# One PSUM bank of row segments for all output terms, and ten projection rows loaded behind the last V block

## The chip, the cores and the metric

The kernel runs on one core of one Trainium2 chip. The metric is the device time of a whole execution in microseconds (us). A "span" is the time from the first to the last instruction of one profiled execution; it is about 1.7 us shorter than the time of the same run. Positions such as "393.2" are microseconds from the start of the span. "Granted clock" is the share of full speed that the profile shows for TensorE's clock: 0.50 is called half clock below. PSUM is the memory in which matmul results accumulate.

## The reference, cut to what matters

One token of a decode step: grouped-query attention over a cache of 65,536 positions, plus an MLP, plus the residual.

```python
def _A_ref(x, k_cache, v_cache, wq, wo):          # x: 1x1x1024, caches: 1x4x65536x128, 32 query heads
    q = (x @ wq) ...
    p = softmax(q @ k * Dh**-0.5)                  # 8 query heads share one K/V head
    o = p @ v
    return o.reshape(B, Sq, 4096) @ wo             # wo: 4096x1024, 32 "rows" of 128x1024, one per query head
def _B_ref(x, w1, w2, w3, w4):
    ... x1 = x + hs                                # w1, w2: 1024x1024
    return x1 + _gelu(_layernorm(x1) @ w3) @ w4    # w4: 3584x1024
x = A_x; xn = _layernorm(x)
return x + _A_ref(xn, ...) + _B_ref(xn, ...)       # 1x1x1024, bf16
```

Nearly all of the work is to read 170 MB once: K and V are 134 MB of it.

## The kernel before

The caches come in 32 blocks (four K/V heads with eight blocks each) of 2 MB of K and 2 MB of V. All loads are issued by SyncE into one queue. Each engine keeps a list of operations, and a small bookkeeping class derives the waits: an operation waits for whoever last wrote what it reads, and for whoever last wrote or read what it writes. It does not ask whether that was the engine itself; the argument below comes back to this.

```python
def _deps(q, reads, writes):
    for b in reads:
        for s, v in b.w.items():
            q.wait((s, v))
    for b in writes:
        for s, v in b.w.items():
            q.wait((s, v))          # also when s is the engine's own semaphore
        for s, v in b.r.items():
            q.wait((s, v))
```

After the last block of a K/V head, `combine_1` and `combine_2` sum and normalise its eight heads into `OTh_bf`. Then each head's vector (128x1) meets its projection row (128x1024), eight matmuls with 128x128 weights and one moving column each:

```python
def wo_pe(h, g, src=None):
    ...
    for ncx in range(KT_D):                        # KT_D = 8
        fns.append(lambda e, ...: e.matmul(OA_ps[:, ncx:ncx + 1], view[:, ncx * P:(ncx + 1) * P], OTh_bf[:, h, g:g + 1],
                                           start=(g == 0 and ncx == 0), stop=(g == G - 1), skip_group_check=True))
    _grp(q_pe, fns, reads=bufs + [b_OTh[h]], writes=[b_OA], partial=(g > 0))
    if g == G - 1:  acc += OA_ps                   # on VectorE
```

The last ten projection rows (two of the third K/V head, all eight of the fourth) load into slots that the MLP's w3 has left free, two for each of blocks 25 to 29. The K and V loads run three blocks ahead, so six of these rows go into the queue ahead of the last K block (issued in block 28). The w4 weights (seven chunks of 1 MB, four 128-row slices each) load last, into freed slots. The end of the program:

```python
for i in range(len(wo_tail)):
    at(min(t_ws_free + i // 2, t0), "dma", lambda i=i: issue_wo_tail_row(i))
... # the 32 blocks, the last combine
for (h_, g_) in wo_tail:
    wo_pe(h_, g_, src=wo_tail_src[(h_, g_)])
mm_interleaved(H2_ps, 0, KT_D, chunks_of("w4"), ...)          # 7 groups of 32 one-column matmuls
fin = acc + H2_ps; transpose fin on TensorE; cast to orow     # 8 partitions x 128
ev_out = _dma(q_sp, ch_out, lambda e: e.dma_start(out=out[0, 0, :].rearrange("(kt p) -> kt p", p=P), in_=orow[:, :]), ...)
```

Of the kernel before, what the change touches and what calls it, by code (L numbers as in the profile page):

```python
# [6 lines left out]
BF = mybir.dt.bfloat16  # L7
F32 = mybir.dt.float32
ACTF = mybir.ActivationFunctionType
ALU = mybir.AluOpType  # L10
# [83 lines left out]
def _op(q, fn, reads=(), writes=(), partial=False):  # L94
    _deps(q, reads, writes)
    ev = q.op(fn, True)
    _done(ev, reads, writes, partial)
    return ev


def _grp(q, fns, reads=(), writes=(), partial=False):
    _deps(q, reads, writes)
    ev = None
    for i, fn in enumerate(fns):
        ev = q.op(fn, i == len(fns) - 1)
    _done(ev, reads, writes, partial)
    return ev
# [8 lines left out]
def _dma(q, chan, fn, reads=(), writes=(), partial=False):  # L116
    _deps(q, reads, writes)
    chan.n += 1
    ev = q.dma(fn, chan.sem, 16 * chan.n)
    _done(ev, reads, writes, partial)  # L120
    return ev
# [10 lines left out]
def bass_parallel_sum__gqa_block_cached__mixer_s_mlp__decode_kernel(  # L132
# [13 lines left out]
    P = 128  # L146
    D = A_x.shape[2]
    HKV, SK, DH = A_k_cache.shape[1], A_k_cache.shape[2], A_k_cache.shape[3]
    HQD = A_wq.shape[1]
    HQ = HQD // DH  # L150
    G = HQ // HKV
    F = B_w3.shape[1]
    KT_D = D // P
# [10 lines left out]
    with ExitStack() as es:  # L164
# [3 lines left out]
        def sb(name, shape, dt):  # L168
            return E(nc.sbuf_tensor(name, shape, dt))

        def ps(name, shape, dt):
            return E(nc.psum_tensor(name, shape, dt))
# [59 lines left out]
        ge_b = sb("ge_b", [P, KT_F], F32)  # L232
        h1g_bf = sb("h1g_bf", [P, KT_D], BF)
        gh_bf = sb("gh_bf", [P, KT_F], BF)
        fin = sb("fin", [P, KT_D], F32)
        orow = sb("orow", [KT_D, P], BF)

        H3_ps = ps("H3_ps", [P, 512], F32)
        H2_ps = H3_ps[:, 32:64]
        OA_ps = ps("OA_ps", [P, 512], F32)  # L240
        S_ps = ps("S_ps", [P, 512], F32)
        PT_ps = ps("PT_ps", [P, 512], F32)
        MBB_ps = ps("MBB_ps", [P, 512], F32)
# [19 lines left out]
        b_Kn = [[_B(), _B()] for _ in range(NK)]  # L263
        b_Vn = [[_B(), _B()] for _ in range(NV)]
        b_X = [[_B() for _ in range(4)] for _ in range(2)]
        b_H3 = _B(); b_H2 = _B(); b_tmpO = [_B(), _B()]
        b_S = _B(); b_PT = _B(); b_MB = _B(); b_OT = _B()
        b_M0 = _B(); b_M1 = _B()
        b_mrow = [_B(), _B()]; b_R = [_B(), _B()]
# [3 lines left out]
        b_Oacc = _B(); b_brun = [_B(), _B()]; b_dd = [_B(), _B()]; b_ff = [_B(), _B()]  # L273
        b_WS = [[_B() for _ in range(4)] for _ in range(NWS)]
        b_wo = [_B() for _ in range(NWO)]
        b_OA = _B()
        b_cb = _B()
        b_OTh = [_B() for _ in range(HKV)]
        b_acc = _B()
# [62 lines left out]
        for kt in range(KT_D):  # L342
# [3 lines left out]
        _op(q_pe, lambda e: e.matmul(M0_ps[:, 160:160 + KT_D], x8[:, :], ident_bf[0:KT_D, 0:KT_D], start=True, stop=True),  # L346
            reads=[b_x8, b_const], writes=[b_M0])
        _op(q_dve, lambda e: e.tensor_copy(xT[:], M0_ps[:, 160:160 + KT_D]), reads=[b_M0], writes=[b_xT])

        ln_uid = [0]  # L350

# [29 lines left out]
        def mm_interleaved(ps_tile, col0, ncols, chunks, rhs_fn, b_rhs, b_ps, kt0=0, nkt_total=None):  # L381
            nkt = nkt_total if nkt_total is not None else sum(c[2] for c in chunks)
            first = (kt0 == 0)
            kt = kt0
            for sl, lhs_fn, kts in chunks:
                fns = []
                for kk in range(kts):
                    for ncx in range(ncols):
                        fns.append(lambda e, kk=kk, ncx=ncx, kt=kt, st=(first and kk == 0 and ncx == 0), lhs_fn=lhs_fn:
                                   e.matmul(ps_tile[:, col0 + ncx:col0 + ncx + 1], lhs_fn(kk, ncx), rhs_fn(kt + kk),  # L390
                                            start=st, stop=(kt + kk == nkt - 1), skip_group_check=True))
                _grp(q_pe, fns, reads=sl.bufs + [b_rhs], writes=[b_ps], partial=not first)
                first = False
                kt += kts
# [152 lines left out]
        def wo_pe(h, g, src=None):  # L547
            if src is None:
                ws_ = (h * G + g) % NWO
                view, bufs = wo_sb[:, ws_, :], [b_wo[ws_]]  # L550
            else:
                view, bufs = src
            fns = []
            for ncx in range(KT_D):
                fns.append(lambda e, ncx=ncx, g=g, h=h, view=view: e.matmul(OA_ps[:, ncx:ncx + 1], view[:, ncx * P:(ncx + 1) * P], OTh_bf[:, h, g:g + 1],  # L555
                                                                          start=(g == 0 and ncx == 0), stop=(g == G - 1), skip_group_check=True))
            _grp(q_pe, fns, reads=bufs + [b_OTh[h]], writes=[b_OA], partial=(g > 0))
            if g == G - 1:
                _op(q_dve, lambda e: e.tensor_tensor(out=acc[:], in0=acc[:], in1=OA_ps[:, 0:KT_D], op=ALU.add), reads=[b_OA, b_acc], writes=[b_acc])

        def mk_loads(name, w, nkt, per):
            ncol = w.shape[1]
# [32 lines left out]
        def chunks_of(name):  # L595
            res = []
            for ld in loads_early + loads_mid + loads_late:
                if ld["name"] != name:
                    continue
                sl, ncol = ld["slot"], ld["ncol"]  # L600
                if name == "w3":
                    res.append((sl, (lambda kk, ncx, sl=sl: sl.view[:, 512 * (ncx // 4) + (ncx % 4): 512 * (ncx // 4) + (ncx % 4) + 4 * P: 4]), 1))
                else:
                    res.append((sl, (lambda kk, ncx, sl=sl, ncol=ncol: sl.view[:, kk * ncol + ncx * P: kk * ncol + (ncx + 1) * P]), ld["kts"]))
            return res

        b_h1 = _B(); b_x1 = _B(); b_xn3 = _B(); b_gh = _B(); b_fin = _B(); b_orow = _B()

        def mlp_early_1():
            mm_interleaved(M1_ps, 64, KT_D, chunks_of("w1"), lambda kt: xn2I_bf[:, kt:kt + 1], b_xn2I, b_M1)  # L610
# [2 lines left out]
        def mlp_early_2():  # L613
            mm_interleaved(M1_ps, 72, KT_D, chunks_of("w2"), lambda kt: g_bf[:, kt:kt + 1], b_const, b_M1)
            _op(q_dve, lambda e: e.tensor_tensor(out=x1[:], in0=xn[:], in1=M1_ps[:, 72:72 + KT_D], op=ALU.add), reads=[b_xn, b_M1], writes=[b_x1])
            _op(q_dve, lambda e: e.tensor_tensor(out=acc[:], in0=acc[:], in1=M1_ps[:, 72:72 + KT_D], op=ALU.add), reads=[b_acc, b_M1], writes=[b_acc])
            layer_norm(x1, b_x1, xn3, xn3_bf, b_xn3)
# [14 lines left out]
        def at(period, slot, fn):  # L632
            pending.setdefault(period, []).append((slot, fn))
# [17 lines left out]
        for i, ld in enumerate(loads_early):  # L651
            at(2 + i // 2, "dma", lambda ld=ld, i=i: issue_load(ld, slots["ws"][i % NWS]))
        at(7, "c", lambda: mlp_early_1())
        at(8, "c", lambda: mlp_early_2())
        for j, ld in enumerate(loads_mid):
            wave, jj = divmod(j, NWS)
            at(10 + 6 * wave + jj, "dma", lambda ld=ld, jj=jj: issue_load(ld, slots["ws"][jj]))
# [8 lines left out]
        def issue_wo_tail_row(i):  # L666
            h_, g_ = wo_tail[i]
            sl = slots["ws"][i // 4]
            j = i % 4
            _dma(q_sp, ch_wot[i], lambda e, sl=sl, j=j, h_=h_, g_=g_: e.dma_start(out=sl.view[:, j * D:(j + 1) * D],  # L670
                                                                                 in_=A_wo[(h_ * G + g_) * DH:(h_ * G + g_ + 1) * DH, :]),
                 writes=[sl.bufs[j]])
            wo_tail_src[(h_, g_)] = (sl.view[:, j * D:(j + 1) * D], [sl.bufs[j]])
            wo_tail_next[0] = max(wo_tail_next[0], i + 1)

        t0 = max(NBLK - KA, NBLK - VA, t_ws_free, 0)
        for i in range(len(wo_tail)):
            at(min(t_ws_free + i // 2, t0), "dma", lambda i=i: issue_wo_tail_row(i))
        at(t0, "dma", lambda: issue_late(slots["ws"][3:4]))
        for n in range(max(0, NBLK - NK), NBLK):  # L680
            at(max(n, t0), "dma", lambda n=n: issue_late(slots["k"][n % NK]))
# [4 lines left out]
        for n in range(NBLK):  # L686
            h, nb = divmod(n, NB)
            issue_k(n + KA)
            issue_v(n + VA)
            run_pending(n, "dma")  # L690
            QK(n)
            Ttr(n + 1, [0])
            stats1(n)
            run_pending(n, "a")
            MB(n)
            stats2(n)
            EXP(n)
            Ttr(n + 1, [1])
            run_pending(n, "b")
            PTr(n)  # L700
            PTevac(n)
            Ttr(n + 1, [2, 3])
            PV(n)
            FLASH(n)
            run_pending(n, "c")
            if nb == NB - 1:
                at(n + 1, "a", lambda h=h: combine_1(h))
                at(n + 1, "b", lambda h=h: combine_2(h))

# [6 lines left out]
                issue_wo_tail_row(i)  # L716
        while late_next[0] < len(loads_late):
            issue_late(slots["ws"])
        for (h_, g_) in wo_tail:
            wo_pe(h_, g_, src=wo_tail_src[(h_, g_)])  # L720
        mm_interleaved(H2_ps, 0, KT_D, chunks_of("w4"), lambda kt: gh_bf[:, kt:kt + 1], b_gh, b_H2)
        _op(q_dve, lambda e: e.tensor_tensor(out=fin[:], in0=acc[:], in1=H2_ps[:, 0:KT_D], op=ALU.add), reads=[b_acc, b_H2], writes=[b_fin])
        _op(q_pe, lambda e: e.transpose(out=M0_ps[0:KT_D, 300:300 + P], in_=fin[:, :], identity=ident_f[:, :]), reads=[b_fin, b_const], writes=[b_M0])
        _op(q_dve, lambda e: e.tensor_copy(orow[:, :], M0_ps[0:KT_D, 300:300 + P]), reads=[b_M0], writes=[b_orow])
        ev_out = _dma(q_sp, ch_out, lambda e: e.dma_start(out=out[0, 0, :].rearrange("(kt p) -> kt p", p=P), in_=orow[:, :]), reads=[b_orow])
        q_sp.wait(ev_out)

        block.sync(lambda e: q_sp.emit(e))
# [32 lines left out]
```

## Time and profile before

| | before |
|---|---|
| time, median of 3 runs | 413.93 us (413.74 to 414.36) |
| span of the profiled run | 412.0 us |
| bytes moved, mean rate | 170 MB, 413 GB/s |
| last K block landed | 376.8 |
| last head's vectors ready | 397.0 |
| last w4 matmul ended | 409.4 |

The page shows the span in 40 equal slices. The first line is the busy share of the DMA engines in tenths, the second the rate in GB/s.

```profile
DMA  7999999999999999999999999999999999999990
GB/s 280 426 435 430 433 429 431 424 437 425 431 433 428 428 429 429 427 421 436 430 426 429 431 425 427 426 433 428 425 431 428 431 429 426 425 422 421 423 387 13
```

The stream of transfers is full all the time, and its end sets a floor. Finer stretches of the end of the stream (stretch, its length, then each engine's busy time, the granted clock of TensorE, the DMA share, GB/s):

```profile
399.50:400.00 0.50, 0.35 (x14) 0.29 (x11) 0.00 (x0) 0.00 (x0) 0.00 (x0) 0.50 0.74 311
401.50:402.00 0.50, 0.50 (x25) 0.50 (x23) 0.16 (x1) 0.00 (x0) 0.00 (x0) 0.50 0.42 180
402.50:403.00 0.50, 0.35 (x15) 0.38 (x15) 0.00 (x0) 0.00 (x0) 0.00 (x0) 0.50 0.00 0
```

The rate falls from 399 on, with the busy share of the 16 DMA engines (0.74, then 0.42), and reaches zero after 402.5. The chain of work that ended last (start, duration, what) tells what comes after:

```profile
352.46 24.32 DMA Kn<-in_A_k_cache_dram
...
394.87 1.88 PE M_ps L543 x8
...
400.66 0.14 issue
400.80 0.36 PE OA_ps L555 x8
...
407.08 0.14 issue
407.21 1.00 PE H_ps L390 x32
...
409.67 0.39 PE M_ps L723
```

The softmax of the last block hangs on the last K block (landed at 352.46 + 24.32 = 376.8). The combine's matmuls (`M_ps`) end at 396.75; ten projection rows (`OA_ps`) follow at 0.36 us and a gap of 0.14 us each, and seven w4 chunks (`H_ps`) at 1.00 and 0.14 us. From 402.5 to the end at 412.0 nothing is transferred but the output. The issuing engine's timeline (start, duration, engine, line, operation) shows where the six rows stand in the queue:

```profile
345.38 6.97 SPq L670 DMA_DIRECT2D WS<-in_A_wo_dram  x2
352.46 3.08 SPq L424 DMA_DIRECT2D Kn<-in_A_k_cache_dram  x1
...
410.39 0.31 SPq L725 DMA_DIRECT2D out_dram<-orow  x1
```

Two rows (the fifth and sixth) were issued directly ahead of the last K block. Their issue took 7 us, against 0.3 to 0.5 us elsewhere; I read this as a full queue.

### The profile page before, as it was taken

Reading aid. Unit: us, or ns where it says so; the run is one execution under the profiler, and the core shown is the slowest. Engines: PE = TensorE matmul, PEld = TensorE weight load, DVE = VectorE, ACT = ScalarE, POOL = GpSimd, SP = SyncE. Lnnn points to the kernel's source line nnn. Section 1 sums busy time; section 2 is a strip of 40 time slices with the busy share of each in tenths; the row PEclk is TensorE's granted clock in tenths of the full one; section 3 lists DMA queues with packets and bytes.
Section 4 is the critical chain, followed back from the end, with each engine's and each line's share of the span. In section 5 each row is a group of like instructions: output and inputs, shape, how many; then the busy total and the mean of one; then the engine's idle time right before and its main releaser. Section 6 shows DMA issues by size and latency. Waiting matters only on the chain.

```text
span 412.0 us, 5690 instructions
## 1 busy us (share of the span) xinstructions
PE 194.8 (47%) x2237; PEld 84.4 (20%) x2237; DVE 226.0 (55%) x401; ACT 48.4 (12%) x127; POOL 61.4 (15%) x88
## 2 busy tenths in 40 slices
PE   1532444434157656424465453445457544333666
PEld 1521111101014312101123121112224111011156
DVE  1037766736476588644456664445666766655400
ACT  0000211201011021110111110011111111011100
POOL 4000011111011121111110011111110111111210
PEclk9999999995555556566555555655555566656555
DMA  7999999999999999999999999999999999999990
GB/s 280 426 435 430 433 429 431 424 437 425 431 433 428 428 429 429 427 421 436 430 426 429 431 425 427 426 433 428 425 431 428 431 429 426 425 422 421 423 387 13
DMA packets 18043, 170.25 MB, mean 413 GB/s; under 512 B 2272, under 2 KB 2272, under 8 KB 7392
## 3 DMA queue, kind: packets, MB, share of 16 engines
q1 hardware_dynamic: 18016, 169.88, 97.5%
q8 instruction: 18, 0.29, 0.3%
q14 instruction: 9, 0.07, 0.0%
HBM read 169.87 MB, written 0.00 MB: 412 GB/s over the span
## 4 chain that ended last, share of the span: by engine, by line
DMA 56%; DVE 18%; PE 11%; SPq 7%; issue 4%; ACT 3%; POOL 1%; POOLq 0%; ACTq 0%; DVEq 0%
DMA Kn<-in_A_k_cache_dram 51%; DVE X L449 10%; DMA X<-in_A_wq_dram 5%; SPq L670 4%; ACT p_sb L491 2%; DVE pT_f L508 2%; DVE mrow L468 2%; PE PT_ps L503 2%; PE S_ps L461 2%; PE H_ps L390 2%; PE M_ps L543 1%; PE OT_ps L516 1%; SPq L436 1%; PE OA_ps L555 1%; SPq L344 1%
## 5 line engine op out<-in xcount | busy, mean ns | idle before, releaser
L449 DVE STREAM_TRANSPOSE X<-Kn 128x1024 f32<-128x1024 f32 x128 | 153.6, 1221 | 104.2 <-DMA Kn<-in_A_k_cache_dram 104.1
L516 PE MATMUL OT_ps<-Vn,pT_f 128*32 128x512 bf16 x512 | 60.7, 627 | 25.9 <-DVE pT_f L508 25.9
L461 PE MATMUL S_ps<-X,Yall 128*32 128x512 bf16 x512 | 59.0, 607 | 11.4 <-DVE X L449 10.1
L474 PE MATMUL MBB_ps<-Rm,Lmat 128*128 128x16 bf16 x32 | 6.2, 195 | 109.8 <-DVE Rm L469 109.8
L530 POOL TENSOR_TENSOR O_acc<-O_acc,tmpO 128x513 f32<-128x513 f32 x28 | 32.9, 1175 | 89.9 <-ACT tmpO L524 89.9
L491 ACT ACTIVATE p_sb<-S_ps,brun 128x512 bf16<-128x512 f32 x32 | 22.0, 687 | 188.9 <-DVE brun L489 168.9
L528 POOL TENSOR_SCALAR O_acc<-O_acc,ff 128x513 f32<-128x513 f32 x28 | 19.5, 698 | 164.0 <-ACT ff L497 164.0
L503 PE MATMUL PT_ps<-p_sb,permR 128*128 128x512 bf16 x32 | 19.2, 600 | 40.0 <-ACT p_sb L491 40.0
L524 ACT ACTIVATE tmpO<-OT_ps 128x512 f32<-128x512 f32 x32 | 19.2, 600 | 108.4 <-PE OT_ps L516 108.4
L474 PEld LDWEIGHTS MBB_ps<-Rm,Lmat 128*128 128x128 bf16 x32 | 3.3, 104 | 134.6 <-DVE Rm L469 134.6
L508 DVE STREAM_TRANSPOSE pT_f<-PT_ps 128x512 f32<-128x512 f32 x32 | 22.9, 717 | 9.8 <-PE PT_ps L503 9.8
L516 PEld LDWEIGHTS OT_ps<-Vn,pT_f 128*32 128x32 bf16 x512 | 14.7, 129 | 58.9 <-DVE pT_f L508 41.9
L461 PEld LDWEIGHTS S_ps<-X,Yall 128*32 128x32 bf16 x512 | 16.0, 125 | 35.6 <-DVE X L449 18.1
L468 DVE TENSOR_REDUCE mrow<-S_ps 128x1 f32<-128x512 f32 x32 | 21.1, 658 | 3.7 <-PE S_ps L461 3.7
L503 PEld LDWEIGHTS PT_ps<-p_sb,permR 128*128 128x128 bf16 x32 | 3.9, 122 | 42.6 <-ACT p_sb L491 42.6
L478 DVE TENSOR_REDUCE Bst<-MBB_ps 128x1 f32<-128x16 f32 x32 | 5.6, 175 | 8.4 <-PE MBB_ps L474 8.4
L555 PEld LDWEIGHTS OA_ps<-OTh_bf,wo_sb 128*128 128x128 bf16 x176 | 6.4, 105 | 18.4 <-issue 18.4
L526 POOL COPY O_acc<-tmpO 128x513 f32<-128x513 f32 x4 | 2.5, 612 | 47.4 <-ACT tmpO L524 47.4
L390 PE MATMUL H_ps<-xn_bf,WS 128*128 128x1 bf16 x224 | 8.6, 172 | 0.0
L555 PE MATMUL OA_ps<-OTh_bf,wo_sb 128*128 128x1 bf16 x176 | 8.2, 168 | 0.0
L390 PEld LDWEIGHTS H_ps<-xn_bf,WS 128*128 128x128 bf16 x224 | 8.1, 117 | 0.0
L543 PE MATMUL M_ps<-cb_W,O_acc 128*128 128x8 f32 x32 | 7.5, 364 | 1.0 <-DVE cb_W L537 1.0
(109 smaller groups left out, 115.2 us busy)
## 6 DMA issues: line engine op xcount, KB each, us to landing
Kn<-in_A_k_cache_dram SPq DMA_DIRECT2D x32, 2048.0 KB, 26.3
Vn<-in_A_v_cache_dram SPq DMA_DIRECT2D x32, 2048.0 KB, 30.7
WS<-in_B_w_dram SPq DMA_DIRECT2D x8, 896.0 KB, 30.5
wo_sb<-in_A_wo_dram SPq DMA_DIRECT2D x22, 256.0 KB, 29.5
WS<-in_B_w_dram SPq DMA_DIRECT2D x5, 1024.0 KB, 30.1
WS<-in_A_wq_dram SPq DMA_DIRECT2D x4, 1024.0 KB, 8.0
X<-in_A_wq_dram SPq DMA_DIRECT2D x4, 1024.0 KB, 16.8
Kn<-in_B_w_dram SPq DMA_DIRECT2D x4, 1024.0 KB, 18.6
```

The costliest lines, as they stand in the source:

```text
L390: e.matmul(ps_tile[:, col0 + ncx:col0 + ncx + 1], lhs_fn(kk, ncx), rhs_fn(kt + kk), start=st, stop=(kt + kk == nkt - 1), skip_group_check= ...
L449: _op(q_dve, lambda e, ix=ix, ks=ks, xs=xs: e.transpose(out=X32[:, xs, 1024 * ix:1024 * (ix + 1)], in_=Kn32[:, ks, 16 * ix:16 * (ix + 1), ...
L461: fns.append(lambda e, we=we, c_mid=c_mid, mv=mv, h=h: e.matmul(S_ps[32 * c_mid:32 * c_mid + 32, :], Yall[:, h, we, :, :].rearrange("p a g ...
L468: _op(q_dve, lambda e, m=m: e.reduce_max(mrow[:, m:m + 1], S_ps[:, :], axis=AX.X), reads=[b_S], writes=[b_mrow[m]])
L491: _op(q_act, lambda e, n=n, m=m, kn=kn: e.activation(p_sb[:, m, :], S_ps[:, :], ACTF.Exp, bias=brun[:, kn:kn + 1], scale=SCALE, accum_out= ...
L503: _op(q_pe, lambda e, m=m: e.matmul(PT_ps[:, :], permR[:, :], p_sb[:, m, :], start=True, stop=True), reads=[b_p[m], b_const], writes=[b_PT])
L508: _op(q_dve, lambda e, m=m: e.transpose(out=pT_f[:, m, :], in_=PT_ps[:, :]), reads=[b_PT], writes=[b_pT[m]])
L516: fns.append(lambda e, q=q, q4=q4, m=m, vs=vs: e.matmul(OT_ps[32 * q4:32 * q4 + 32, :], pT_bf[:, m, q, :, 1], Vn[:, vs, 4 * q:4 * q + 4, : ...
L524: _op(q_act, lambda e, m=m: e.activation(tmpO[:, m, 0:512], OT_ps[:, :], ACTF.Copy), reads=[b_OT], writes=[b_tmpO[m]], partial=True)
L528: _op(q_pool, lambda e, m=m: e.tensor_scalar(out=O_acc[:, :], in0=O_acc[:, :], scalar1=ff[:, m, 0:1], scalar2=0.0, op0=ALU.mult, op1=ALU.add),
L530: _op(q_pool, lambda e, m=m: e.tensor_tensor(out=O_acc[:, :], in0=O_acc[:, :], in1=tmpO[:, m, :], op=ALU.add), reads=[b_tmpO[m]], writes=[ ...
L555: fns.append(lambda e, ncx=ncx, g=g, h=h, view=view: e.matmul(OA_ps[:, ncx:ncx + 1], view[:, ncx * P:(ncx + 1) * P], OTh_bf[:, h, g:g + 1] ...
```

## The change

The intent: get the last K block earlier, as more work hangs on it than on the projection rows; and let every output term (residual, 32 projection rows, 28 slices of w4) accumulate in one PSUM bank, as four row segments of 256 columns on partitions 0, 32, 64 and 96, so that the final add, transpose and small cast go. For this weight and moving operand change places: the head's vector is the one-column weight, and the projection row moves.

```diff
+        _op(q_dve, lambda e: e.memset(OUT_ps[:, :], 0.0), writes=[b_OUT])
+        def out_rows(items, reads, last=False):
+            fns = []
+            for lhs, view in items:
+                for jj in range(4):
+                    st = not out_started[0]
+                    fns.append(lambda e, ...: e.matmul(
+                        OUT_ps[32 * jj:32 * jj + 1, 0:256], lhs, view[:, 256 * jj:256 * jj + 256],
+                        start=st, stop=last, tile_position=(0, 32 * jj), skip_group_check=True))
+                out_started[0] = True
+            _grp(q_pe, fns, reads=reads, writes=[b_OUT], partial=True)
+        def out_resid():  ... # eight f32 matmuls put the residual and x1 into the bank, in block 8
     ... # wo_pe:
-            for ncx in range(KT_D): ... OA_ps ...
-            if g == G - 1: acc += OA_ps
+            out_rows([(OTh_bf[:, h, g:g + 1], view)], bufs + [b_OTh[h]])
     ...
-            at(min(t_ws_free + i // 2, t0), "dma", lambda i=i: issue_wo_tail_row(i))
+            at(NBLK - KA - 1, "dma", lambda i=i: issue_wo_tail_row(i))     # all ten in block 28, behind the last V
     ...
+        for (h_, g_) in wo_tail[0:2]:  wo_pe(...)          # the two rows of the earlier head
+        combine_1(HKV - 1); combine_2(HKV - 1)
+        for (h_, g_) in wo_tail[2:]:   wo_pe(...)
+        for i in range(len(w4_ch)):    w4_pe(i)            # out_rows with four slices, a group for each chunk
-        fin = acc + H2_ps; transpose; cast of 8x128
+        _op(q_dve, lambda e: e.tensor_copy(orow[:, :], OUT_ps[:, 0:256]), reads=[b_OUT], writes=[b_orow])
+        ... dma_start(out=out[0, 0, :].rearrange("(j n) -> j n", j=4), in_=orow[0:97:32, :])
```

More of the change, by code (lines that the diff above doesn't have):

```diff
@@ L234, in bass_parallel_sum__gqa_block_cached__mixer_s_mlp__decode_kernel @@
         gh_bf = sb("gh_bf", [P, KT_F], BF)
-        fin = sb("fin", [P, KT_D], F32)
-        orow = sb("orow", [KT_D, P], BF)
+        orow = sb("orow", [P, 256], BF)
         H3_ps = ps("H3_ps", [P, 512], F32)
-        H2_ps = H3_ps[:, 32:64]
-        OA_ps = ps("OA_ps", [P, 512], F32)
+        OUT_ps = ps("OUT_ps", [P, 512], F32)
         S_ps = ps("S_ps", [P, 512], F32)
@@ L265, in bass_parallel_sum__gqa_block_cached__mixer_s_mlp__decode_kernel @@
         b_X = [[_B() for _ in range(4)] for _ in range(2)]
-        b_H3 = _B(); b_H2 = _B(); b_tmpO = [_B(), _B()]
+        b_H3 = _B(); b_tmpO = [_B(), _B()]
         b_S = _B(); b_PT = _B(); b_MB = _B(); b_OT = _B()
@@ L275, in bass_parallel_sum__gqa_block_cached__mixer_s_mlp__decode_kernel @@
         b_wo = [_B() for _ in range(NWO)]
-        b_OA = _B()
+        b_OUT = _B()
         b_cb = _B()
@@ L348, in bass_parallel_sum__gqa_block_cached__mixer_s_mlp__decode_kernel, with out_resid @@
         _op(q_dve, lambda e: e.tensor_copy(xT[:], M0_ps[:, 160:160 + KT_D]), reads=[b_M0], writes=[b_xT])
+        _op(q_dve, lambda e: e.memset(OUT_ps[:, :], 0.0), writes=[b_OUT])
+        out_started = [False]
+        def out_rows(items, reads, last=False):
[3 more added lines that the diff above has]
+                    st = not out_started[0]
+                    fns.append(lambda e, lhs=lhs, view=view, jj=jj, st=st, last=last: e.matmul(
+                        OUT_ps[32 * jj:32 * jj + 1, 0:256], lhs, view[:, 256 * jj:256 * jj + 256],
+                        start=st, stop=last, tile_position=(0, 32 * jj), skip_group_check=True))
+                out_started[0] = True
+            _grp(q_pe, fns, reads=reads, writes=[b_OUT], partial=True)
+        def out_resid():
+            fns = []
+            for kt in range(KT_D):
+                jj, half = divmod(kt, 2)
+                fns.append(lambda e, kt=kt, jj=jj, half=half: e.matmul(
+                    OUT_ps[32 * jj:32 * jj + 1, half * P:(half + 1) * P], acc[:, kt:kt + 1], ident_f[:, :],
+                    start=(half == 0), stop=False, tile_position=(0, 32 * jj), skip_group_check=True))
+            assert not out_started[0]
+            out_started[0] = True
+            _grp(q_pe, fns, reads=[b_acc, b_const], writes=[b_OUT], partial=True)
         ln_uid = [0]
@@ L552, in wo_pe @@
                 view, bufs = src
-            fns = []
-            for ncx in range(KT_D):
-                fns.append(lambda e, ncx=ncx, g=g, h=h, view=view: e.matmul(OA_ps[:, ncx:ncx + 1], view[:, ncx * P:(ncx + 1) * P], OTh_bf[:, h, g:g + 1],
-                                                                          start=(g == 0 and ncx == 0), stop=(g == G - 1), skip_group_check=True))
-            _grp(q_pe, fns, reads=bufs + [b_OTh[h]], writes=[b_OA], partial=(g > 0))
-            if g == G - 1:
-                _op(q_dve, lambda e: e.tensor_tensor(out=acc[:], in0=acc[:], in1=OA_ps[:, 0:KT_D], op=ALU.add), reads=[b_OA, b_acc], writes=[b_acc])
+            out_rows([(OTh_bf[:, h, g:g + 1], view)], bufs + [b_OTh[h]])
         def mk_loads(name, w, nkt, per):
@@ L605, in chunks_of @@
             return res
-        b_h1 = _B(); b_x1 = _B(); b_xn3 = _B(); b_gh = _B(); b_fin = _B(); b_orow = _B()
+        b_h1 = _B(); b_x1 = _B(); b_xn3 = _B(); b_gh = _B(); b_orow = _B()
         def mlp_early_1():
@@ L653, in bass_parallel_sum__gqa_block_cached__mixer_s_mlp__decode_kernel @@
         at(7, "c", lambda: mlp_early_1())
-        at(8, "c", lambda: mlp_early_2())
+        at(8, "c", lambda: (mlp_early_2(), out_resid()))
         for j, ld in enumerate(loads_mid):
@@ L705, in bass_parallel_sum__gqa_block_cached__mixer_s_mlp__decode_kernel @@
             run_pending(n, "c")
-            if nb == NB - 1:
+            if nb == NB - 1 and n + 1 < NBLK:
                 at(n + 1, "a", lambda h=h: combine_1(h))
@@ L718, in bass_parallel_sum__gqa_block_cached__mixer_s_mlp__decode_kernel, with w4_pe @@
             issue_late(slots["ws"])
-        for (h_, g_) in wo_tail:
-            wo_pe(h_, g_, src=wo_tail_src[(h_, g_)])
-        mm_interleaved(H2_ps, 0, KT_D, chunks_of("w4"), lambda kt: gh_bf[:, kt:kt + 1], b_gh, b_H2)
-        _op(q_dve, lambda e: e.tensor_tensor(out=fin[:], in0=acc[:], in1=H2_ps[:, 0:KT_D], op=ALU.add), reads=[b_acc, b_H2], writes=[b_fin])
-        _op(q_pe, lambda e: e.transpose(out=M0_ps[0:KT_D, 300:300 + P], in_=fin[:, :], identity=ident_f[:, :]), reads=[b_fin, b_const], writes=[b_M0])
-        _op(q_dve, lambda e: e.tensor_copy(orow[:, :], M0_ps[0:KT_D, 300:300 + P]), reads=[b_M0], writes=[b_orow])
-        ev_out = _dma(q_sp, ch_out, lambda e: e.dma_start(out=out[0, 0, :].rearrange("(kt p) -> kt p", p=P), in_=orow[:, :]), reads=[b_orow])
+        w4_ch = chunks_of("w4")
+        def w4_pe(i):
+            sl, _, kts = w4_ch[i]
+            kt = sum(c[2] for c in w4_ch[:i])
+            out_rows([(gh_bf[:, kt + kk:kt + kk + 1], sl.view[:, kk * D:(kk + 1) * D]) for kk in range(kts)],
+                     sl.bufs + [b_gh], last=(i == len(w4_ch) - 1))
+        for (h_, g_) in wo_tail[0:2]:
+            wo_pe(h_, g_, src=wo_tail_src[(h_, g_)])
+        combine_1(HKV - 1)
+        combine_2(HKV - 1)
+        for (h_, g_) in wo_tail[2:]:
+            wo_pe(h_, g_, src=wo_tail_src[(h_, g_)])
+        for i in range(len(w4_ch)):
+            w4_pe(i)
+        _op(q_dve, lambda e: e.tensor_copy(orow[:, :], OUT_ps[:, 0:256]), reads=[b_OUT], writes=[b_orow])
+        ev_out = _dma(q_sp, ch_out, lambda e: e.dma_start(out=out[0, 0, :].rearrange("(j n) -> j n", j=4), in_=orow[0:97:32, :]), reads=[b_orow])
         q_sp.wait(ev_out)
```

## The prediction

> **What bounds the kernel now.** The memory stream, until about 402 us: over the page's slices the 16 DMA engines are busy throughout at about 425 GB/s up to 399 us; in half-microsecond stretches the rate then tapers off (311, 246, 180, 66 GB/s) and is zero from 402.5 us. It moves 170 MB, which the change leaves alone. Behind it hangs a tail on TensorE. By the chain of waits: the last K block landed at 376.8; its PV ends at 391.8; GpSimd's accumulation ends at 393.7; combine ends at 396.95; ten projection rows (0.36 us of matmuls, 0.14 us gap each) end at 401.65; seven w4 chunks (1.00 us, 0.14 us gap each) end at 409.4; add, transpose and cast take 1.0 us, the output store 1.6 us. So TensorE starts w4 when its data has all but landed: some 7 us overlap no transfer.
>
> **What the change does.**
> 1. Six of the ten 256 KB rows were issued ahead of the last K block; now they follow the last V block. Six rows are 1.57 MB, at 425 GB/s 3.7 us. The last K block should land at about 373.1, and what hangs on it (PV, combine) come 3.7 us earlier: combined heads ready at 393.2. The stream's end stays at about 402: same bytes, and the queue is deep (18 to 24 us from issue to landing), so waits of the issuing engine shouldn't drain it.
> 2. A row was eight matmuls of one column with 128x128 weights; now it is four of 256 columns with one-column weights, on four column tiles. The Trainium skill ("TensorE: Matmul & The Clock Gate", Part 3) says that tiles of the array run concurrently; this trace agrees: sixteen 512-column matmuls on four tiles take 1.90 us, 0.43 us per four, where a lone one takes 0.61. Half the columns should need 0.21 to 0.25 us per row at the same granted clock (0.50). w4: 0.25 to 0.285 before, so little changes; projection rows go from 0.50 to about 0.37 with their gap.
> 3. Two rows of the earlier head move ahead of the combine, into TensorE's wait.
> 4. The final add, transpose and small cast (1.0 us) become one 128x256 cast, estimated 0.42 us from the 0.28 us of the 128-column one.
> 5. Added: a PSUM memset and eight f32 matmuls early on, hidden by the stream.
>
> **The new tail.** Combine done 393.2; eight rows x 0.37 to 396.2; seven chunks x 1.0 to 403.2. The last chunk lands at about 402 and then needs 0.5 to 1.0 us, so the stream's limit (403) and TensorE's nearly coincide. Plus 0.07, cast 0.42, store 1.65: span about 405.3 against 412.0. Gain 6.7 us, 1.6%: 407.2 us. The floor is the end of the stream: to pass 2% (405.7 us) that end itself would have to move.
>
> **Checks in the profile.** Last K block landing near 373; DMA ending near 402; heads ready near 393; a four-matmul row at 0.21 to 0.25 us; last matmul at 403; cast near 0.4 us; TensorE waiting on the last w4 transfers, or just short of it.
>
> **What would make it wrong.** Tiles that don't overlap: 0.85 us per row would add 20 us, slower. Weight loads that don't hide: 0.35 us per row costs some 4 us. The granted clock rising in a denser tail: w4 then waits for the stream, gaining at most 0.5 us. Late rows stalling or draining the queue: the stream's end shifts.
>
> Chances: faster by over 2% 0.12, within 2% 0.82, slower by over 2% 0.06. Range 405.6 to 409.6.

## The result, and the profile after

The changed kernel took 408.84 us in the median of 4 runs (408.25 to 409.52), the kernel before 413.86 us in the median of 4. The ratio is 0.9877 (95% interval 0.9858 to 0.9896): the gain is 5.0 us or 1.2%, where 6.7 us was predicted. (Ratios here are the mean time of one kernel's fast runs over that of the other's of the same rounds, so not quite the ratio of the medians.) The slices of the page:

```profile
DMA  7999999999999999999999999999999999999993
GB/s 275 429 429 435 431 434 421 435 432 424 430 434 428 429 429 427 421 431 437 429 425 431 422 428 429 430 433 426 426 431 426 425 432 427 431 430 425 408 425 159
```

The stream is as full as before. Its end has not moved:

```profile
401.50:402.00 0.50, 0.50 (x16) 0.14 (x4) 0.00 (x0) 0.00 (x0) 0.00 (x0) 0.50 0.39 164
402.50:403.00 0.50, 0.50 (x16) 0.27 (x8) 0.00 (x0) 0.00 (x0) 0.00 (x0) 0.50 0.00 0
```

The chain of work that ended last:

```profile
349.15 23.75 DMA Kn<-in_A_k_cache_dram
...
390.99 1.89 PE M_ps L566 x8
...
393.07 0.14 issue
393.21 0.41 PE OUT_ps L356 x4
...
397.58 1.05 PE OUT_ps L356 x16
398.63 0.14 issue
...
404.15 0.14 issue
404.29 0.64 PE OUT_ps L356 x16
404.92 0.02 issue
404.94 0.43 DVE orow L752
```

The last K block lands at 372.9 instead of 376.8, and the heads are ready at 393.07 instead of 396.95: 3.9 us, where 3.7 was predicted. But a projection row of four matmuls takes 0.41 us and a gap of 0.14, 0.55 in all: more than the old row of eight (0.50), and far more than the predicted 0.37. So TensorE ends at 404.92, about two microseconds after the stream. The issuing engine's timeline:

```profile
349.15 0.33 SPq L447 DMA_DIRECT2D Kn<-in_A_k_cache_dram  x1
...
350.48 25.92 SPq L687 DMA_DIRECT2D WS<-in_A_wo_dram  x10
...
405.40 0.61 SPq L753 DMA_DIRECT2D out_dram<-orow  x1
```

The ten rows now stand behind the last K and V. Their issue blocks SyncE for 26 us, which costs nothing, as the transfers stay busy (the slices above). The store at the end is shown with 0.61 us at its issue, against 0.31 before, and the span ends 2.1 us after that issue began, against 1.6. The list of waits of TensorE from 385 us on (who waited for whom: total us, times, longest) names what stands between the groups:

```profile
PE OUT_ps L356 <- PE OUT_ps L356: 2.6, 16, 0.2
```

TensorE waits sixteen times for itself.

### The profile page after: what moved, and what is told of

It is laid out like the page before. It is cut to its first block, busy times and chain, and to the rows that moved or that the text cites. A ratio compares the mean times of both kernels' runs of the same rounds, so it can differ in the third digit from the quotient of the medians.

```text
span 407.5 us, 5235 instructions
## 1 busy us (share of the span) xinstructions
PE 194.4 (48%) x2012; PEld 76.6 (19%) x2012; DVE 225.9 (55%) x397; ACT 48.4 (12%) x127; POOL 61.5 (15%) x88
## 4 chain that ended last, share of the span: by engine, by line
DMA 62%; DVE 18%; PE 11%; issue 3%; ACT 3%; SPq 1%; POOL 0%; POOLq 0%; ACTq 0%; DVEq 0%
DMA Kn<-in_A_k_cache_dram 57%; DVE X L472 10%; DMA X<-in_A_wq_dram 5%; PE OUT_ps L356 2%; ACT p_sb L514 2%; DVE pT_f L531 2%; DVE mrow L491 2%; PE PT_ps L526 2%; PE S_ps L484 2%; PE M_ps L566 1%; PE M_ps L413 1%; PE OT_ps L539 1%; SPq L342 1%; DVE Yall L426 1%; DVE Rm L492 1%
## 5 line engine op out<-in xcount | busy, mean ns | idle before, releaser
L356 PE MATMUL OUT_ps<-wo_sb,OTh_bf 128*1 128x256 bf16 x88 | 9.5, 421 | 0.0
```

The costliest lines, as they stand in the source:

```text
L356: fns.append(lambda e, lhs=lhs, view=view, jj=jj, st=st, last=last: e.matmul(OUT_ps[32 * jj:32 * jj + 1, 0:256], lhs, view[:, 256 * jj:256 ...
```

## The experiments

The theories. **A**: the order of the transfers gives most of the gain. Its rival **B**: the stream is saturated, so the order of its bytes is nothing, and the gain is that of the output path. **C**: what the prediction missed is a fixed cost of each group of matmuls, because a group waits for the semaphore of the last matmul of the group before. Its rival **D**: any wait, or the short matmul itself, costs this.

### e1: only the rows moved

In the kernel before, the one line of the row loads:

```diff
-            at(min(t_ws_free + i // 2, t0), "dma", lambda i=i: issue_wo_tail_row(i))
+            at(NBLK - KA - 1, "dma", lambda i=i: issue_wo_tail_row(i))
```

> The kernel before with one line changed: all ten late projection rows are issued behind the last V block, the output path stays as before. Theory A (the order of the transfers gives nearly all of the gain, because the softmax chain of the last block hangs on the last K block): last K block lands at about 373 instead of 376.8 us, heads ready at about 393.1, then the old ten rows and seven w4 chunks take the same 12.4 us as before, so last matmul at about 405.5; span about 408.1, about 3.9 us faster than the kernel before. Rival B (the stream is saturated, so the order of its bytes changes nothing and the gain is that of the output path): within 1 us of the kernel before.

Measured: 411.02 us in the median (410.78 to 412.58, 6 runs), ratio 0.9939 (0.9925 to 0.9954); span 409.1, 2.9 us less. The chain of e1:

```profile
349.08 23.85 DMA Kn<-in_A_k_cache_dram
...
403.35 0.40 PE H_ps L390 x10
403.76 0.74 issue
404.50 0.76 PE H_ps L390 x22
```

The last K block lands at 372.9, as A said, so B falls. Of the expected 3.9 us one is missing, and the trace shows where: a w4 chunk, 1.00 us elsewhere, was cut in two by a gap of 0.74 us in which TensorE waited for nothing that the profile shows. What it was stays open, but the trace holds a hint. The program's instructions come by DMA too, in packets of 16 KB on a queue of their own (q8). In e1 such a packet moved from 402.3 to 403.2, when about 190 matmuls and weight loads were still to start; in the kernel before, whose TensorE program is the same, it came with about 330 left. The profile of e5 below (the kernel before but for its store) has a gap of the same kind (0.21 us, up to 403.3) and such a late packet too (about 480 left, not 580). Each gap ended 1.2 to 1.3 us after its packet. So TensorE may have run out of instructions; no run tests it. Two of the six runs were 1.3 to 1.6 us slower than the others; whether for the same reason the trace of another run cannot say.

### e2: only the output path

The changed kernel with the row loads at their old places (the diff of e1 reversed).

> The changed kernel with the ten projection rows issued at their old places: only the output path is changed. Theory A: last K block lands at 376 to 377 us as before, heads ready at about 397, eight rows at 0.54 us and seven w4 chunks at 1.0 to 1.2 us end at 408.6 to 409.4, cast and store 2.5 us: 0.5 to 1.3 us faster than the kernel before. Rival B: nearly the whole gain of the change, about 5 us. The two runs e1 and e2 should add up to the gain of the change, 5.0 us, if the parts are independent.

Measured: 412.97 us (412.02 to 414.16, 6 runs), ratio 0.9978 (0.9964 to 0.9993); span 410.5. The last K block in the chain of e2, and the last w4 chunk in its timeline:

```profile
352.49 24.32 DMA Kn<-in_A_k_cache_dram
```

```profile
407.36 0.61 PE L356 MATMUL OUT_ps<-Vn,gh_bf 128*1 128x256 bf16 x16 [0.16 <-PE OUT_ps L356]
```

A was right here too: the block lands at 376.8 as before, and the gain is about 1 us. But in the profiled run that gain is one of the clock: the last four chunks ran at full clock (0.61 us instead of 1.02), which saves 1.6 us, so that the last matmul ended at 408.0 and not at 408.6 or later as expected. Of the profiled spans, e1 gains 2.9 and e2 1.5 us, together 4.4, and the change 4.5 (412.0 to 407.5). By the mean ratios the parts give 2.5 and 0.9 us, together 3.4, and the change 5.1 (4.3 in e8). That they add up is thus shown to 1 or 2 us only; e1 had lost about 1 us in its gap. The order of the transfers is the larger part.

### e3: without the wait of TensorE for itself

```diff
+            own = b_OUT.w.pop(q_pe.sem, None)        # forget the own last write
             _grp(q_pe, fns, reads=reads, writes=[b_OUT], partial=True)
```

> The changed kernel, with TensorE no longer waiting, ahead of each group of output matmuls, for its own previous group (the program's bookkeeping makes an engine wait for its own last write[...]). The waits for transfers and for the heads stay. Theory C (each group pays about 0.34 us beyond its 0.213 us per row: 0.20 of emptying the pipe because the next group waits for the semaphore of the last matmul, and 0.14 until the next starts): a row in the tail goes from 0.54 to 0.21 to 0.25 us, w4 chunks that have landed follow at about 0.85 to 0.9 us, TensorE then waits for the last transfer (about 402.3 us) and its last matmul ends at 403.1 to 403.5 instead of 404.9: about 1.5 us faster than the changed kernel, 6.5 us (1.6%) faster than the kernel before. Rival D (any wait, even for a transfer that has long landed, or the latency of a short matmul itself, makes the gap): rows stay at about 0.5 us and the time is that of the changed kernel within 0.5 us.

Measured: 408.51 us (408.31 to 408.71, 4 runs), ratio 0.9868 (0.9853 to 0.9882). The timeline of e3:

```profile
393.18 1.88 PE L356 MATMUL OUT_ps<-WS,OTh_bf 128*1 128x256 bf16 x32 [0.35 <-DVE OTh_bf L569]
394.83 1.07 PE L356 MATMUL OUT_ps<-WS,gh_bf 128*1 128x256 bf16 x16
...
400.56 1.02 PE L356 MATMUL OUT_ps<-Vn,gh_bf 128*1 128x256 bf16 x16 [1.87 <-DMA Vn<-in_B_w_dram]
403.00 1.02 PE L356 MATMUL OUT_ps<-Vn,gh_bf 128*1 128x256 bf16 x16 [1.42 <-DMA Vn<-in_B_w_dram]
```

All eight rows took 1.88 us (0.235 each; 32 matmuls), although each still waits for its own, long landed, transfer; the result stayed correct. So C holds for the mechanism and D falls. The size is less sure: expected was 1.5 us below the changed kernel, measured 0.3 from median to median (of different rounds), 0.9 from span to span. The changed kernel did not run in these rounds, and e8 (409.85) would make it 1.3, so how much it gains stays open. The kernel before waits for itself in the same way (0.14 us between its groups); what it would gain without that was not run either. The tail has turned into a wait for the stream: TensorE idles 1.87 and 1.42 us ahead of the last two chunks, and the chain of e3 ends on the last transfer:

```profile
381.07 21.88 DMA Vn<-in_B_w_dram
```

That landed at 402.95, not at 402.3 as I had read from the rates, and the last chunk ran at half clock (1.02 us instead of the 0.61 of warm ones).

### e4: the eight rows in one group, self-waits kept elsewhere

```diff
-        for (h_, g_) in wo_tail[2:]:
-            wo_pe(h_, g_, src=wo_tail_src[(h_, g_)])
+        out_rows([... the eight rows ...], [... all their buffers ...] + [b_OTh[HKV - 1]])
```

> The changed kernel, with the eight rows of the last head put into one group of 32 matmuls with all waits ahead of the first; everything else, the self-waits ahead of each w4 chunk too, is kept. Theories C and D agree here: the eight rows take 8 x 0.213 + 0.34, about 2.05 us, instead of 4.35. The seven w4 chunks stay at 1.19 us (0.77 when the granted clock is full), the last one held by its transfer: last matmul at about 403.5, 1.3 us faster than the changed kernel. If instead the row itself is slow (weight loads of one column that don't hide, 0.4 us each), the 32 matmuls take 3.5 us or more.

Measured: 408.23 us (408.11 to 408.67, 4 runs), ratio 0.9861 (0.9846 to 0.9875). The timeline of e4:

```profile
392.92 1.88 PE L356 MATMUL OUT_ps<-WS,OTh_bf 128*1 128x256 bf16 x32 [0.35 <-DVE OTh_bf L568]
394.95 1.02 PE L356 MATMUL OUT_ps<-WS,gh_bf 128*1 128x256 bf16 x16 [0.16 <-PE OUT_ps L356]
396.14 0.61 PE L356 MATMUL OUT_ps<-Kn,gh_bf 128*1 128x256 bf16 x16 [0.16 <-PE OUT_ps L356]
...
403.04 1.02 PE L356 MATMUL OUT_ps<-Vn,gh_bf 128*1 128x256 bf16 x16 [1.83 <-DMA Vn<-in_B_w_dram]
```

The same 1.88 us by another way: the one-column weights do hide. The last matmul ended at 404.1, not at 403.5, held by the last transfer as in e3.

### e5: a store of four rows in the kernel before (wrong result on purpose)

```diff
-... out=out[0, 0, :].rearrange("(kt p) -> kt p", p=P), in_=orow[:, :]
+... out=out[0, 0, :].rearrange("(kt p) -> kt p", p=P)[0:4, :], in_=orow[0:4, :]
```

> The kernel before, with the output store cut to four of its eight rows of 256 bytes (wrong result on purpose: half of the output is never written). In the changed kernel and in e2 to e4 the store of four rows of 512 bytes shows 0.61 us at its issue and the span ends 2.03 to 2.1 us after that issue started; in the kernel before and e1 the store of eight rows of 256 bytes shows 0.31 us and ends 1.62 to 1.67 us after. Theory E (the number of rows[...] sets it): four rows show 0.61 us and end about 2.05 us after the issue here too. Rival F (the step of 32 partitions in the source or the 512-byte rows set it): 0.31 us and 1.65 us as before.

Measured, one look: 414.09 us beside 414.03 of before. Its timeline:

```profile
410.81 0.29 SPq L725 DMA_DIRECT2D out_dram<-orow  x1
```

The span ended at 412.4, 1.6 us after that start. My theory E, the number of rows, falls; the step of 32 partitions or the row's size is left (e9, e10).

### e6: the last w4 chunk in two transfers

The kernel of e3, with the last chunk's load split by columns into two transfers with a semaphore each, and its group of matmuls split likewise.

```diff
-        for i in range(len(w4_ch)):
+        for i in range(len(w4_ch) - 1):
             w4_pe(i)
+        for hh in range(2):                         # two slices behind each half's own semaphore
+            out_rows([... slices 2*hh and 2*hh + 1 of the last chunk ...], [half buffer hh, b_gh], last=(hh == 1))
```

> The kernel of e3 (no self-wait), with the last w4 chunk brought by two transfers with a semaphore each, so that two rows instead of four remain for TensorE after the last landing. Theory G (with the self-waits gone, the end hangs on the landing of the last transfer at about 403.0 us, and only what follows it counts): the last group takes about 0.6 us instead of 1.02, last matmul at about 403.65 instead of 404.04, 0.4 us faster than e3. Rival H (TensorE still sets the end): no change, or slower by the extra group's cost of 0.1 us or more.

Measured: 408.32 us (408.07 to 408.46, 4 runs), ratio 0.9858 (0.9844 to 0.9871). From timeline and chain of e6:

```profile
403.57 0.60 PE L356 MATMUL OUT_ps<-Vn,gh_bf 128*1 128x256 bf16 x8 [0.64 <-DMA Vn<-in_B_w_dram]
```

```profile
382.38 21.15 DMA Vn<-in_B_w_dram
```

From the last landing to the end of the last matmul it is 0.64 us (403.53 to 404.17) instead of 1.07 in e3 (402.95 to 404.02): the 0.4 us expected. The landing itself came 0.6 us later in this profiled run, and the intervals of e3 and e6, of different rounds, overlap, so the times don't show the gain. This run's heads were ready only at 393.9, 0.8 us later than in e3, and the tail still waited for transfers: theory G, the end hangs on the stream.

### e7: TensorE kept busy while it waits

The kernel of e6 with sixteen 512-column matmuls into an unused bank ahead of each of the last two chunks.

```diff
             w4_pe(i)
+            if i >= len(w4_ch) - 3:
+                filler(16)        # results are never read
```

> The kernel of e6, with two groups of sixteen 512-column matmuls into an unused PSUM bank put into TensorE's waits for the last two transfers. In e3 the granted clock had fallen back to 0.50 for the last chunk (1.02 us for 16 matmuls, against 0.61 at the full clock). If the fall comes from the idle time ahead of it, the last group of 8 matmuls should run at a clock of 1.0 and take about 0.4 instead of 0.6 us, 0.2 us faster than e6 at most; if the fillers run at the half clock they take 1.9 us each and may make the last group late by up to 0.9 us, and the kernel is slower than e6.

Measured: 407.98 us (407.83 to 407.99, 5 runs), ratio 0.985 (0.9836 to 0.9863). The timeline of e7:

```profile
401.24 1.04 PE L765 MATMUL M_ps<-WS,ident_bf 128*32 128x512 bf16 x16
402.10 0.39 PE L356 MATMUL OUT_ps<-Vn,gh_bf 128*1 128x256 bf16 x8
403.27 0.39 PE L356 MATMUL OUT_ps<-Vn,gh_bf 128*1 128x256 bf16 x8 [0.78 <-DMA Vn<-in_B_w_dram]
```

The groups of eight took 0.39 us instead of 0.60: the clock stayed at full (granted clock 1.00 from 401.5 to 403.7). In the same rounds e7 is 0.3 us below e6, and no run of one overlaps the other, though the intervals of the ratios do. This is the fastest version: 6.0 us or 1.5% under the kernel before in these rounds.

### e8: the changed kernel again

> The changed kernel itself, on the same chip and in the same rounds as e6 and e7. Its first four runs spread from 408.25 to 409.52 us, more than the 0.6 us of the kernel before. If the spread comes from the moment at which the granted clock rises in the tail (a w4 chunk takes 1.19 us with its gap at half clock and 0.77 at full), the profile shows a different number of slow chunks than the five of the first profile; otherwise five again.

Measured: 409.85 us (409.32 to 410.33, 4 runs), ratio 0.9895 (0.9882 to 0.9909), 1.0 us above the first look at the same kernel. The last chunk of e8, in its timeline:

```profile
404.34 1.02 PE L356 MATMUL OUT_ps<-Vn,gh_bf 128*1 128x256 bf16 x16 [0.16 <-PE OUT_ps L356]
```

All seven chunks were slow here (1.02 us), where the first profile had the last two at 0.61. So the moment at which the clock rises moves the end: two chunks are 2 x 0.41 = 0.8 us. It also shows what the new output path gives by itself. From the heads' being ready to the end of the span the profiles show 15.05 us in the kernel before, 15.2 in e8 (no fast chunk), 14.4 in the first profile of the changed kernel (two fast chunks) and 13.5 in e2 (four). At half clock throughout, the new path with its self-waits saves nothing; in the profiles of the kernel before and of e1 the clock never rose in the tail. Why it rises sooner in one run than in another was not tested. Against this kernel in the same rounds, e6 is 1.5 us faster (the ratios differ by 0.9895 - 0.9858, times 414 us) and e7 1.9 us (0.9895 - 0.985).

### e9 and e10: the store

The kernel of e7, its store from neighbouring partitions (e9) or with half rows (e10), wrong results on purpose.

```diff
-in_=orow[0:97:32, :]
+in_=orow[0:4, :]                                                  # e9
+out=...[:, 0:128], in_=orow[0:97:32, 0:128]                       # e10
```

> The kernel of e7 with the output store taken from four neighbouring partitions (0 to 3) in place of 0, 32, 64 and 96 (wrong result on purpose). e5 showed that the number of rows does not matter: 0.29 us at the issue and 1.6 us to the end. Theory J (the step of 32 partitions in the source costs the extra 0.3 to 0.4 us): 0.3 us at the issue and about 1.65 us from issue to the end here. Rival K (rows of 512 bytes cost it): 0.61 and about 2.05 us as in e7.

> The kernel of e7 with the output store cut to the first half of each row, 256 bytes, from partitions 0, 32, 64 and 96 (wrong result on purpose). Theory J (the step): 0.61 us at the issue and about 2.05 us to the end as in e7. Rival K (the row's size): 0.3 and about 1.65 us.

Measured, one look each: 407.69 us (span 406.0) and 407.93 us (span 406.2). The store in e9, then in e10:

```profile
404.38 0.29 SPq L780 DMA_DIRECT2D out_dram<-orow  x1
```

```profile
404.17 0.61 SPq L780 DMA_DIRECT2D out_dram<-orow  x1
```

From the start of the issue to the end it is 1.6 us in e9 and 2.0 in e10. So the step of 32 partitions costs the 0.3 us at the issue and 0.4 in all, not the rows' size or number (one profile each, but all seven profiles with the step and full rows show 0.61, and the three of before, e1 and e5 0.29 to 0.31). It comes with the layout: the four column tiles write to partitions 0, 32, 64 and 96.

## Why the prediction was right, and where its sizes were off

The time (408.84) lies in the range (405.6 to 409.6) and the direction and mechanism were right; the gain came out at 5.0 of 6.7 us. That it came so near is in part luck: the clock rose for the last two chunks, which saved 0.8 us, and the same kernel (e8, 409.85) lies just outside the range. Point by point, for the profiled run (span 407.5, predicted 405.3):

- **Transfer order (point 1): right.** Landing 372.9 (said 373.1), heads ready 393.07 (said 393.2). e1 confirms the landing with this part alone. The end of the stream stayed. Read as the landing of the last transfer it is 402.95 to 403.5 (e3, e6), somewhat later than the 402 that I read from the falling rates.
- **Cost of a row (point 2): the term that was mis-sized.** The tiles overlap as said: in e3 a row costs 0.235 us. The Trainium skill ("TensorE: Matmul & The Clock Gate", Part 3) says that tiles run concurrently, and this agrees. But "projection rows go from 0.50 to about 0.37 with their gap" left out that each group also has to run empty. At half clock a group takes 0.21 us for each row plus 0.2, and then 0.14 until the next starts: 0.41 + 0.14 for one row, 1.05 + 0.14 for four. The page's section "Single matmul latency" gives a lone matmul on the full array some 183 ns at the cold clock on top of its columns. By this a row of four tiles would take about 0.40 us (an estimate from that figure: 0.21 + 0.18); measured was 0.41. The eight rows took 4.4 instead of 3.0 us, the chunks 7.5 instead of 7.0 (8.3 in e8, where none was fast).
- **The wait behind it.** I had read the 0.14 us "issue" as unavoidable. It comes from TensorE waiting for its own semaphore, which e3 took away.
- **Final cast (point 4): right** (0.43, said 0.42).
- **The store: mis-sized.** "Store 1.65" became 2.1; e9 and e10 show the step of 32 partitions as the cause.
- **The sum.** Rows 1.4, chunks 0.5 and store 0.45 make 2.35 us, less 0.1 for the earlier heads: the 2.2 us by which the span missed.
- **The floor: right.** "The floor is the end of the stream": with the groups' cost gone (e3, e4) the end moves by less than that cost, as TensorE then waits for transfers. Even e7 stays within 2% of the kernel before.

## What to carry to other kernels

In a full stream of loads, the order decides what is exposed at the end: put first the bytes with the longest chain of work behind them (3.9 us here for six small rows moved, no byte saved). A helper that makes an engine wait for its own last write costs little between large groups and more than the work itself between small ones (0.34 us here, on 0.21 us of work); cost a small group as columns plus a fixed part, and look in the list of waits for an engine that waits for itself. Once the tail reaches the end of the stream, only what follows the last landing counts, so make the last transfer small and the work behind it short.

## What the Trainium skill lacked or had wrong

- "TensorE: Matmul & The Clock Gate": Part 2 has the latency of a lone matmul, but no page that I read says what a wait for the engine's own semaphore between accumulating groups costs: 0.34 us a group at half clock (eight rows in 4.4 us with it, 1.88 without).
- The same page, Part 1: the clock is said to rise after about 3.4 us of sustained activity. In e4, after 1.88 us without a gap and one chunk, it had risen about 3 us into the tail (chunks of 1.02, then 0.61 us). In the changed kernel, with TensorE busy some 70% of the time in the rows and 86 to 88% in the chunks, and a gap after each group, it rose only after 10 us (first profile) or not within the 12 us of the tail (e8); in e2, with the same gaps, after 8. The page doesn't say what share of busy time counts as sustained.
- "DMA: Bandwidth & Descriptors": its breakdown of the fixed cost, which is for transfers issued by GpSimd, calls descriptor generation "small, variable"; this store is issued by SyncE. No page that I read gives the cost of a stepped partition source for a small store: 0.61 against 0.29 us at the issue, about 0.4 us in all (e9, e10).
